# Transposing q, k and u by DMA in place of TensorE, with the sink loads on GpSimd's queue

## Chip, cores and metric

The kernel runs on one core of one Trainium2 chip. The metric is the device time of one execution in microseconds. A run counts as slow when it is over 1.5% above the fastest run of the same kernel. The engines are named as the profile names them: PE (TensorE), DVE (VectorE), ACT (ScalarE), POOL (GpSimd), SP (the queue of SyncE). To issue a DMA is to put it into a queue; it lands when its data have arrived.

## The reference

Attention with a sliding window of 128 and four sink tokens, followed by one MLP-Mixer block.

```python
# q, k, v: (batch 4, heads 8, seq 768, head_dim 64), float32
scores = scale * q @ k^T
keep = (key < 4) | ((query - key >= 0) & (query - key < 128))
x = softmax(where(keep, scores, -1e9)) @ v      # to (batch, 768, 512)
h  = relu(x^T @ w_tok1) @ w_tok2
u  = x + h^T
out = u + relu(u @ w_ch1) @ w_ch2
```

## The kernel before

Each batch has two groups of four heads (groups 0 to 7). PE runs the channel matmuls of batch b, called C1 and C2 here. The attention and the token mixing of batch b+1 are woven into them at fixed places of PE's program. Three operands must be transposed: q, k, and u, which C1 reads as `uT`. PE does all of that through PSUM, the memory in which PE's results stand, and ACT or DVE copies the result out; such a copy is called an eviction here.

```python
def load_qk(eng, src, dst, G, lo, hi):       # partition p holds tokens 6p..6p+5: rows of 1536 bytes
    return eng.dma_start(
        out=dst[:, lo:hi].rearrange("p h t d -> p h (t d)"),
        in_=src[G.b, G.h0 + lo:G.h0 + hi].rearrange("h (p t) d -> p h (t d)", t=NT))

def load_sinks():                            # four small loads on ACT's queue
    for h in range(GH):
        nc.scalar.dma_start(out=vs_f[4 * h:4 * h + 4, :, h, 0:D],
                            in_=v.rearrange("b (a h) s d -> h s (b a) d", h=GH)[h, 0:4])

def tr(j, which):                            # q or k of two heads: six PE transposes, one copy
    ps = ps_ms.tile([P, NT, P], BF16, name="ps_tr", tag="ms")
    for t in range(NT):
        nc.tensor.transpose(ps[:, t], src[:, j, t].rearrange("p i d -> p (i d)"), ident)
    ...
def utr(st):                                 # one 128-row block of u: four PE transposes, one copy
    ps = ps_ms.tile([P, NC, P], BF16, name="ps_ut", tag="ms")
    for c in range(NC):
        nc.tensor.transpose(ps[:, c], u_sb[:, st, ts(c, P)], ident)
    nc.scalar.activation(uT[:, :, ts(st, P)], ps, AF.Copy)

def prep_v(g):
    cast_v(held[g])
    if g + 2 < NG and g >= 2:
        fetch(g + 2)                         # loads of q, k, v for two groups later, on the SP queue
...
            # (cut) towards the end of batch b's channel matmuls:
            fill += [(mid + 0.01, lambda n=n: prep_qk(n)) for n in (h + 1, h + 2)]
            fill += [(mid + 0.01, lambda n=n: prep_v(n)) for n in (h + 1, h + 2)]
            hi = mid + 0.03                  # then token mixing and the transposes of u for batch b+1
            fill += [(hi + (0.97 - hi) * n / (len(nhead) - 1), f) for n, (f, _) in enumerate(nhead)]
```

The first half of C1 of a batch reads only the first three of the six blocks of `uT`.

The softmax here doesn't subtract the row's maximum and nothing guards it: scores larger than these inputs give would overflow.

## Time and profile before

| | |
|---|---|
| time, median | 242.3 us |
| PE busy, share of the span | 218.0 us, 91% |
| ACT, DVE, POOL busy | 43%, 47%, 38% |
| DMA packets, bytes | 39315, 29.40 MB |

The view by stretches gives the stretch and its length in us, the busy time of PE, of PE's weight loads, of DVE, ACT and POOL (with the number of instructions), then the granted PE clock as a share of full speed, the busy share of the DMA engines as the profile counts it, which can pass 1, and the rate in GB/s. From 80 us on PE is busy nearly all the time (two of the stretches are shown); at the start it is not.

```profile
7.00:12.00 5.00, 0.51 (x6) 0.34 (x6) 1.39 (x6) 1.68 (x2) 4.06 (x8) 0.60 1.11 345
12.00:19.00 7.00, 6.50 (x39) 3.03 (x40) 2.20 (x5) 3.48 (x5) 4.63 (x7) 0.56 1.20 189
...
90.00:100.00 10.00, 9.97 (x65) 5.20 (x64) 5.31 (x8) 2.83 (x6) 1.62 (x3) 1.00 1.15 319
100.00:110.00 10.00, 10.00 (x85) 5.86 (x82) 5.29 (x11) 7.47 (x12) 1.73 (x2) 1.00 0.82 203
```

The timeline of ACT (start, duration, engine, line, what) shows why the start is slow. The four sink-load issues hold ACT for 7.62 us, and its first cast of k comes only at 11.60 us. (The bracket calls these 10.30 us idle, since the profile does not count issues as busy.)

```profile
2.66 7.62 ACTq L127 DMA_DIRECT2D vs_f<-in_v_dram  x4
10.30 1.28 ACT L119 ACT_TABLE_LOAD   x1 [10.30 <-POOL qb L116]
11.60 0.84 ACT L119 ACTIVATE kb<-k_113 128x768 bf16<-128x768 f32 x1
```

The timeline of PE at the passage from batch 0 to batch 1 shows what a set of PE transposes costs. The six transposes of line 193 push the next C1 matmuls from 101.37 to 101.70 us, that is 0.33 us. Sets of four transposes of u, read in the same way a little earlier, cost 0.22 to 0.23 us.

```profile
101.37 0.50 PE L193 MATMUL ps_tr<-ident,qb 128*128 128x128 bf16 x6
101.70 0.81 PE L321 MATMUL ps_v<-uT,w_ch_103 128*128 128x384 bf16 x4
```

The timeline of the SP queue just before that passage is a list of DMA issues. Six loads for groups 6 and 7 are issued from 87.38 to 96.6 us.

```profile
87.38 0.39 SPq L98 DMA_DIRECT2D q_1238<-in_q_dram  x1
87.86 0.53 SPq L98 DMA_DIRECT2D k_1239<-in_k_dram  x1
90.19 0.37 SPq L122 DMA_DIRECT2D v_1242<-in_v_dram  x1
90.61 4.77 SPq L98 DMA_DIRECT2D q_1249<-in_q_dram  x1
95.43 0.55 SPq L98 DMA_DIRECT2D k_1250<-in_k_dram  x1
96.08 0.51 SPq L122 DMA_DIRECT2D v_1253<-in_v_dram  x1
```

### The profile page before, as it was taken

The page shows a single profiled execution, that of the slowest core. Times are in us where ns is not written, and L with a number is a line of the kernel's source. Part 1 is how long each engine was busy: PE and PEld are TensorE (multiplying, and loading weights), DVE is VectorE, ACT ScalarE, POOL GpSimd, SP SyncE. Part 2 cuts the span into 40 slices and gives each one's busy share as a digit, 9 for nine tenths or more (in the row PEclk, how much of TensorE's full clock was granted, in tenths as well). Part 3 has the DMA queues.
Part 4 walks back from the last instruction along what each step waited for, and adds up shares of the span by engine and source line. Part 5 has one row for each costly group of instructions (what it writes and reads, how often), then busy time and mean ns, then how long its engine had stood idle before and what let it go on. Part 6 is the DMA issues. An engine that isn't in the chain of part 4 may idle for free.

```text
span 240.4 us, 4233 instructions
## 1 busy us (share of the span) xinstructions
PE 218.0 (91%) x1733; PEld 121.6 (51%) x1733; DVE 113.6 (47%) x251; ACT 103.6 (43%) x162; POOL 91.3 (38%) x126
## 2 busy tenths in 40 slices
PE   6099895899889989999999999998999999999993
PEld 2044373355455654554565644655566555554441
DVE  3325566335475455562563645633556444333331
ACT  0248833343978412478572212596761123321100
POOL 6669407000498992018279900047390000000000
PEclk9659999799999999999999999999999999999999
DMA  6999999989207999990010112100001021101122
GB/s 221 350 214 143 209 329 207 301 156 284 90 0 141 316 263 311 326 222 0 3 44 3 44 44 76 59 0 3 17 29 44 3 87 44 45 3 44 44 89 87
DMA packets 39315, 29.40 MB, mean 122 GB/s; under 512 B 25664, under 2 KB 35648, under 8 KB 39296
## 3 DMA queue, kind: packets, MB, share of 16 engines
q1 hardware_dynamic: 33744, 20.71, 32.5%
q0 software_dynamic: 4448, 7.08, 13.3%
q10 hardware_dynamic: 1104, 1.34, 1.6%
q8 instruction: 13, 0.21, 0.4%
q14 instruction: 6, 0.05, 0.1%
HBM read 26.77 MB, written 6.29 MB: 138 GB/s over the span
## 4 chain that ended last, share of the span: by engine, by line
PE 67%; DVE 9%; issue 6%; DMA 6%; ACT 5%; POOL 4%; ACTq 0%; DVEq 0%; POOLq 0%
PE ps_w L333 26%; PE ps_v L321 21%; PE ps_u L309 4%; ACT pT L225 4%; DMA v_116<-in_v_dram 3%; PE ps_h L302 3%; PE ps_s L219 3%; DMA k_113<-in_k_dram 3%; PE ps_tr L193 3%; PE ps_ut L315 2%; DVE o L336 2%; DVE u_sb L310 2%; PE ps_o L257 1%; DVE qT L113 1%; PE ps_o L252 1%
## 5 line engine op out<-in xcount | busy, mean ns | idle before, releaser
L321 PE MATMUL ps_v<-uT,w_ch_103 128*128 128x384 bf16 x384 | 75.3, 328 | 2.3 <-ACT uT L316 0.7
L321 PEld LDWEIGHTS <-w_ch_103 128*128 128x128 bf16 x384 | 35.2, 98 | 29.3 <-issue 10.2
L225 ACT ACTIVATE pT<-ps_s 128x1024 bf16<-128x1024 f32 (+1 forms) x48 | 43.7, 962 | 8.0 <-PE ps_s L219 7.8
L229 POOL TENSOR_TENSOR pT<-pT,mask_92 128x512 bf16<-128x512 bf16 x12 | 13.8, 1152 | 65.4 <-ACT pT L225 65.4
L336 DVE TENSOR_TENSOR o<-ps_w,u_sb 128x512 f32<-128x512 f32 x24 | 16.6, 692 | 29.1 <-PE ps_w L333 29.0
L316 ACT ACTIVATE uT<-ps_ut 128x512 bf16<-128x512 bf16 x24 | 14.0, 596 | 34.1 <-PE ps_ut L315 34.1
L310 DVE TENSOR_TENSOR u_sb<-ps_u,x_b 128x512 bf16<-128x512 f32 x24 | 16.3, 687 | 21.8 <-PE ps_u L309 21.8
L236 POOL TENSOR_SCALAR_AFFINE_SELECT pT<-pT 128x640 bf16<-128x640 bf16 x24 | 18.3, 762 | 6.5 <-ACT pT L225 6.5
L270 DVE TENSOR_TENSOR x_b<-ps_o,rc 128x256 bf16<-128x256 f32 x42 | 17.8, 425 | 1.4
L333 PE MATMUL ps_w<-w_ch_104,v_111 128*128 128x512 bf16 x72 | 18.3, 379 | 0.0
L333 PE MATMUL ps_w<-w_ch_104,v_574 128*128 128x512 bf16 x72 | 18.3, 379 | 0.0
L333 PE MATMUL ps_w<-w_ch_104,v_1361 128*128 128x512 bf16 x72 | 18.3, 379 | 0.0
L113 DVE COPY qT<-ps_tr 128x768 bf16<-128x768 bf16 x16 | 15.3, 955 | 4.8 <-PE ps_tr L193 4.6
L219 PE MATMUL ps_s<-qT,kT 64*128 64x256 bf16 x192 | 15.7, 269 | 0.9 <-ACT pT L225 0.8
L333 PE MATMUL ps_w<-w_ch_104,v_2040 128*128 128x512 bf16 x72 | 16.0, 379 | 0.0
L239 POOL TENSOR_SCALAR_AFFINE_SELECT pT<-pT 128x512 bf16<-128x512 bf16 x24 | 15.5, 648 | 0.0
L257 PEld LDWEIGHTS <-pT 128*128 128x128 bf16 x192 | 13.9, 98 | 2.9 <-issue 0.4
L119 ACT ACTIVATE kT<-ps_tr 128x768 bf16<-128x768 bf16 x14 | 11.3, 809 | 8.7 <-PE ps_tr L193 8.6
L302 PE MATMUL ps_h<-x_b,w_tok_101 128*128 128x256 bf16 x96 | 13.4, 272 | 1.0 <-DVE x_b L270 0.5
L257 PE MATMUL ps_o<-va,pT 128*128 128x65 bf16 x168 | 14.3, 194 | 0.0
L269 DVE RECIPROCAL rc<-ps_o 128x4 f32<-128x4 f32 x42 | 7.5, 178 | 13.7 <-PE ps_o L261 8.4
L324 ACT ACTIVATE v_2040<-ps_v 128x384 bf16<-128x384 f32 x12 | 5.9, 490 | 16.9 <-PE ps_v L321 16.2
(125 smaller groups left out, 298.8 us busy)
## 6 DMA issues: line engine op xcount, KB each, us to landing
out_dram<-o SPq DMA_DIRECT2D x23, 256.0 KB, 2.3
w_ch_103<-in_moe_w_ch_dram POOLq DMA_DIRECT2D x2, 768.0 KB, 10.1
w_ch_104<-in_moe_w_ch_dram POOLq DMA_DIRECT2D x2, 768.0 KB, 18.9
k_113<-in_k_dram ACTq DMA_DIRECT2D x2, 384.0 KB, 5.5
q_112<-in_q_dram SPq DMA_DIRECT2D x2, 384.0 KB
q_118<-in_q_dram SPq DMA_DIRECT2D x2, 384.0 KB, 8.1
v_116<-in_v_dram SPq DMA_DIRECT2D x1, 768.0 KB, 7.9
v_122<-in_v_dram SPq DMA_DIRECT2D x1, 768.0 KB, 9.8
```

The source lines that it names most:

```text
L113: nc.vector.tensor_copy(out=o, in_=i)
L219: nc.tensor.matmul(ps[:, i, at:at + w], G.kT[j][ds(64 * i, 64), ts(kt, P)], G.qT[j][ds(64 * i, 64), ds(kt * P, w)], start=not first, stop= ...
L225: nc.scalar.activation(pT[:, :, 512 * u:512 * u + n], ps[:, :, 0:n], AF.Exp, scale=scale)
L236: nc.gpsimd.affine_select(out=cur, in_=cur, compare_op=ALU.is_ge, fill=0.0, base=0, pattern=[[0, NT - 1], [1, P]], channel_multiplier=-1)
L239: nc.gpsimd.affine_select(out=prv, in_=prv, compare_op=ALU.is_ge, fill=0.0, base=-1, pattern=[[0, NT - 2], [-1, P]], channel_multiplier=1)
L257: nc.tensor.matmul(o, pT[:, i, ds(256 * qt, P)], G.va[:, h, qt], start=(qt < 2 and h == 0), stop=(h == GH - 1 and qt == 0), skip_group_che ...
L270: nc.vector.tensor_tensor(out=x_b[:, qt, c0:c0 + GH * D].rearrange("p (h d) -> p h d", h=GH), in0=o[:, :, 0:D], in1=rc.to_broadcast([P, GH ...
L302: nc.tensor.matmul(ps, w_tok1[:, t, ts(tt, P)], x_b[:, t, ds(a * GH * D, GH * D)], start=(t == 0), stop=(t == NT - 1))
L310: nc.vector.tensor_tensor(out=u_sb[:, st], in0=ps, in1=x_b[:, st], op=ALU.add)
L321: nc.tensor.matmul(ps, w_ch1[:, c, ts(ft, P)], uT[:, c, ds(half * HS, HS)], start=(c == 0), stop=(c == NC - 1))
L333: nc.tensor.matmul(ps, v1[:, ft, ts(st, P)], w_ch2[:, ft], start=(ft == 0), stop=(ft == NF - 1))
L336: nc.vector.tensor_tensor(out=o, in0=ps, in1=u_sb[:, st], op=ALU.add)
```

## The change

The intent is to take 168 transposes (96 of q and k, 72 of u) and their PSUM copies off PE, ACT and DVE, and to free ACT at the start. The PSUM copy also put the tokens of q and k into order; the DMA transpose, as it is written here, does not. So q and k of groups 4 to 7 are now loaded as 256-byte rows, in the layout that v always had. (Not shown below: the tiles of qT and kT now hold a whole group, with two buffers in place of three.)

```diff
+        G.dma = g >= 2 * GB
 def load_qk(eng, src, dst, G, lo, hi):
-            in_=src[G.b, G.h0 + lo:G.h0 + hi].rearrange("h (p t) d -> p h (t d)", t=NT))
+            in_=src[G.b, G.h0 + lo:G.h0 + hi].rearrange("h (p t) d -> p h (t d)", t=NT)
+        ) if not G.dma else eng.dma_start(
+            out=dst.rearrange("p h t d -> p (h t) d"),
+            in_=src[G.b, G.h0:G.h0 + GH].rearrange("h (t p) d -> p (h t) d", p=P))
...
+    def cast_and_turn(G, which, copy):
+        (cut: one cast on POOL to bf16, token block outermost)
+        nc.sync.dma_start_transpose(out=T, in_=flat)
...
 def load_sinks():
-            nc.scalar.dma_start(
-                out=vs_f[4 * h:4 * h + 4, :, h, 0:D],
+            nc.gpsimd.dma_start(out=vs_c[4 * h:4 * h + 4],
...
 def cast_sinks(lo, hi):      # the zeros of vsink now come from a small mask dm
-        nc.vector.tensor_copy(out=vsink[0:4 * GH, lo:hi], in_=vs_f[:, lo:hi])
+        for h in range(GH):
+            nc.vector.tensor_scalar(out=vsink[0:4 * GH, lo:hi, h, 0:D], in0=vs_c[:, lo:hi],
+                scalar1=dm[:, h], scalar2=None, op0=ALU.mult)
+            nc.vector.tensor_copy(out=vsink[0:4 * GH, lo:hi, h, D:D1],
+                in_=dm[:, h:h + 1].to_broadcast([4 * GH, hi - lo, 1]))
...
+        def sink_keys(j):       # used in place of tr() for groups 4 to 7
+            for i in range(2):
+                nc.scalar.activation(kz[j][ds(64 * i, 64), ds(8 * j + 4 * i, 4)],
+                                     G.T[1][j][ds(64 * i, 64), 0, 0:4], AF.Copy)
...
 def utr(st):
+            if b > 0:
+                nc.sync.dma_start_transpose(out=uT[:, :, ts(st, P)], in_=u_sb[:, st])
+                return
...
+                order += [(lambda g=g: begin(g), 0)] + ([(lambda h=h: begin(h), 0)] if b > 0 else [])
+                if held[g].dma:
+                    order += [(step(x, 0, i), 0) for x in (g, h) for i in range(2)]
```

The last lines put the sink-key copies of both groups at the start of batches 1 and 2 (for the attention of batches 2 and 3).

More of the change, by code (lines that the diff above doesn't have):

```diff
@@ L50 @@
     bfp = ctx.enter_context(tc.tile_pool(name="bfp", bufs=2))
-    att = ctx.enter_context(tc.tile_pool(name="att", bufs=3))
+    att = ctx.enter_context(tc.tile_pool(name="att", bufs=2))
     ptp = ctx.enter_context(tc.tile_pool(name="ptp", bufs=4))
@@ L65 @@
     ks = [[singles.tile([P, P], BF16, name=f"ks{a}{j}") for j in range(2)] for a in range(2)]
-    vs_f = singles.tile([4 * GH, NG, GH, D1], FP32, name="vs_f")
+    dm = singles.tile([4 * GH, GH, 1], FP32, name="dm")
+    vs_c = singles.tile([4 * GH, NG, D], FP32, name="vs_c")
     vsink = singles.tile([P, NG, GH, D1], BF16, name="vsink")
@@ L92, in tiles @@
         G.va = bfp.tile([P, GH, NT, D1], BF16, name="va")
-        G.qT, G.kT, G.pT = [None, None], [None, None], [None, None]
+        G.T, G.pT = [None, None], [None, None]
         return G
@@ L110, in cast @@
         copy(dst[:, j].rearrange("p t i d -> p i t d"), src[:, 2 * j:2 * j + 2])
+    def cast_and_turn(G, which, copy):
+        src, dst = ((G.q32, G.qb), (G.k32, G.kb))[which]
+        flat = dst.rearrange("p j t i d -> p (j t i d)")
+        copy(flat.rearrange("p (t h d) -> p t h d", t=NT, h=GH), src.rearrange("p h t d -> p t h d"))
+        T = att.tile([P, 2 * NT, P], BF16, name="qT" if which == 0 else "kT")
+        nc.sync.dma_start_transpose(out=T, in_=flat)
+        G.T[which] = [T.rearrange("d (t j) p -> d t j p", j=2)[:, :, j] for j in range(2)]
     def by_dve(o, i):
@@ L126, in load_sinks @@
         for h in range(GH):
-            nc.scalar.dma_start(
-                out=vs_f[4 * h:4 * h + 4, :, h, 0:D],
-                in_=v.rearrange("b (a h) s d -> h s (b a) d", h=GH)[h, 0:4])
+            nc.gpsimd.dma_start(out=vs_c[4 * h:4 * h + 4],
+                                in_=v.rearrange("b (a h) s d -> h s (b a) d", h=GH)[h, 0:4])
     def load_tok():
@@ L166, in build_sinks @@
     def build_sinks():
-        one = vs_f[:, :, :, D]
-        nc.gpsimd.memset(one, 1.0)
+        nc.gpsimd.memset(dm, 1.0)
         nc.gpsimd.affine_select(
-            out=one, in_=one, compare_op=ALU.is_ge, fill=0.0,
-            base=0, pattern=[[0, NG], [-4, GH]], channel_multiplier=1)
+            out=dm[:, :, 0], in_=dm[:, :, 0], compare_op=ALU.is_ge, fill=0.0,
+            base=0, pattern=[[-4, GH]], channel_multiplier=1)
         nc.gpsimd.affine_select(
-            out=one, in_=one, compare_op=ALU.is_ge, fill=0.0,
-            base=3, pattern=[[0, NG], [4, GH]], channel_multiplier=-1)
+            out=dm[:, :, 0], in_=dm[:, :, 0], compare_op=ALU.is_ge, fill=0.0,
+            base=3, pattern=[[4, GH]], channel_multiplier=-1)
     def cast_sinks(lo, hi):
-        nc.vector.tensor_copy(out=vsink[0:4 * GH, lo:hi], in_=vs_f[:, lo:hi])
+        for h in range(GH):
+            nc.vector.tensor_scalar(
+                out=vsink[0:4 * GH, lo:hi, h, 0:D], in0=vs_c[:, lo:hi],
+                scalar1=dm[:, h], scalar2=None, op0=ALU.mult)
+            nc.vector.tensor_copy(
+                out=vsink[0:4 * GH, lo:hi, h, D:D1],
+                in_=dm[:, h:h + 1].to_broadcast([4 * GH, hi - lo, 1]))
     def cast_v(G):
@@ L193, in tr @@
                 nc.tensor.transpose(ps[:, t], src[:, j, t].rearrange("p i d -> p (i d)"), ident)
-            dst = att.tile([P, S], BF16, name="qT" if which == 0 else "kT")
+            if j == 0:
+                T = att.tile([P, 2 * NT, P], BF16, name="qT" if which == 0 else "kT")
+                G.T[which] = [T[:, NT * x:NT * x + NT] for x in range(2)]
+            dst = G.T[which][j].rearrange("d t p -> d (t p)")
             (by_act if which and (g >= GB or j == g) else by_dve)(
                 dst.rearrange("d (p t) -> d p t", t=NT), ps.rearrange("d t p -> d p t"))
-            if which == 0:
-                G.qT[j] = dst
-            else:
-                G.kT[j] = dst
+            if which == 1:
                 for i in range(2):
@@ L219, in sc @@
                     nc.tensor.matmul(
-                        ps[:, i, at:at + w],
-                        G.kT[j][ds(64 * i, 64), ts(kt, P)], G.qT[j][ds(64 * i, 64), ds(kt * P, w)],
+                        ps[:, i, at:at + w].rearrange("p (c q) -> p c q", q=P),
+                        G.T[1][j][ds(64 * i, 64), kt], G.T[0][j][ds(64 * i, 64), kt:kt + w // P],
                         start=not first, stop=not first or at > 0, skip_group_check=first)
@@ L245, in sk @@
             for j in range(2):
-                nc.tensor.matmul(ps, kz[j], G.qT[j][:, 2 * P:S], start=(j == 0), stop=(j == 1))
+                nc.tensor.matmul(ps.rearrange("p (c q) -> p c q", q=P), kz[j], G.T[0][j][:, 2:NT], start=(j == 0), stop=(j == 1))
             G.pk = small.tile([P, 512], BF16, name="pk")
@@ L284, in pv2 @@
                 in0=o[:, :, :, 0:D], in1=rc.to_broadcast([P, 2, GH, D]), op=ALU.mult)
-        T = [lambda j=j, w=w: tr(j, w) for j in range(2) for w in range(2)]
+        if G.dma:
+            T = [lambda j=j: sink_keys(j) for j in range(2)]
+        else:
+            T = [lambda j=j, w=w: tr(j, w) for j in range(2) for w in range(2)]
         Sc = [lambda j=j, u=u: sc(j, u) for j in range(2) for u in range(3)]
@@ L393, in prep_qk @@
         def prep_qk(g, by=(by_pool, by_pool)):
+            if held[g].dma:
+                for which in range(2):
+                    cast_and_turn(held[g], which, by_pool)
+                return
             for j in range(2):
@@ L413 @@
         parts[1] = attention(1, G1, xs[0], True)
-        nc.gpsimd.memset(vs_f, 0.0)
         load_q(G0, 0, 2)
@@ L420 @@
         load_k(G1, 0, 2, nc.scalar)
-        load_sinks()
         nc.vector.memset(warm, 0.0)
@@ L428 @@
         build_masks()
+        load_sinks()
+        build_sinks()
         nc.vector.memset(vsink, 0.0)
@@ L462 @@
         seq += [C(G1, 0, 0, by_pool), C(G1, 0, 1, by_pool), I(1), step(0, 1, 3), step(1, 0, 0), step(0, 1, 4)]
-        seq += [step(1, 0, 1), step(0, 1, 5), step(1, 1, 0), build_sinks]
+        seq += [step(1, 0, 1), step(0, 1, 5), step(1, 1, 0)]
         seq += [C(G1, 1, 0, by_pool), C(G1, 1, 1, by_pool), step(0, 2, 0), step(1, 0, 2), step(1, 1, 1), step(1, 0, 3)]
@@ L482 @@
                     order += [(lambda: prep_qk(2), 0)]
-                order += [(lambda g=g: begin(g), 0)]
-                order += [(step(g, 0, i), 8) for i in range(4)]
+                order += [(lambda g=g: begin(g), 0)] + ([(lambda h=h: begin(h), 0)] if b > 0 else [])
+                if held[g].dma:
+                    order += [(step(x, 0, i), 0) for x in (g, h) for i in range(2)]
+                else:
+                    order += [(step(g, 0, i), 8) for i in range(4)]
                 for n in range(3):
@@ L489 @@
                     order += [(lambda: prep_qk(3, (by_dve, by_act)), 0)]
-                order += [(lambda h=h: begin(h), 0)]
-                order += [(step(h, 0, i), 8) for i in range(4)]
+                order += [(lambda h=h: begin(h), 0)] if b == 0 else []
+                if not held[h].dma:
+                    order += [(step(h, 0, i), 8) for i in range(4)]
                 if b == 0:
```

## The prediction

> **What bounds the kernel now.** TensorE is 91% busy (page); PE holds 67% of the chain of waits. The stretch view shows PE busy 9.1 to 10 of every 10 us from 80 to 230 us, at full clock. Before that it is not PE alone: from 7.7 to 12.5 us PE waits for ACT's first cast of k, and ACT was idle until 10.3 us because its four sink-load issues (timeline, 2.66 to 10.28 us) blocked it; PE then ran at clock 0.5 until 19 us.
>
> **Removed.** 96 PE transposes of q and k, 72 of u. The groups view books about 90 ns each, but in the timeline six delay the next matmul by 0.33 us (101.37 to 101.70), four by about 0.22. So 16 x 0.33 + 18 x 0.22 = about 9.3 us of PE time, nearly all on the critical path: 1.3 us before batch 1's channel matmuls, 8 after. The evictions that go were hidden. Moving the sink loads lets PE restart about 4 us earlier; the split sink casts on DVE give some back: 3.5 us net.
>
> **Added.** q and k of groups 4 to 7 are loaded as 256-byte rows, as v is. By the stretch view v loads run at about 218 GB/s (10 to 18 us), the old q/k loads at 390 (80 to 82 us): 3.6 us for 768 KB in place of 2.0. Loads, DMA transposes and stores sit on the SP queue in program order: before batch 1's u transposes come three stores, four q/k transposes (waiting for GpSimd's casts), then six loads for groups 6 and 7. In the old trace the third store ends at 87.3 us, the casts at 88.6, and the faster loads last until 107 us. PE's u transposes needed no DMA; now they do. The Trainium skill, "DMA: Bandwidth & Descriptors" (Two DMAs through the same engine are not ordered), says descriptors of one queue start in order; the old trace agrees in that one SP load issue took 4.77 us behind others.
>
> Estimate: casts done at 86 us; four transposes 6 to 8 us of queue (same page, Latency and other measured facts, 261 GB/s: 1.5 us per 384 KB; no transpose is in the old trace); six loads 21.6 us; a store and three u transposes: uT lands at about 116 us. PE would be ready at 100.7 - 3.5 - 1.3 = 96 us, and waits for exactly those three u transposes. Stall 20 us, plus 2 for a clock drop after it. Batches 2 and 3 have no loads queued and 4 to 5 us of slack: little stall.
>
> Sum: 242.3 - 9.3 - 3.5 + 20 + 2 = about 251; I say 249.
>
> **Prediction: 249 us, 231 to 264 in 8 of 10; faster 0.2, same 0.14, slower 0.66.**
>
> **What would show it.** PE idle 10 to 25 us once, near 96 to 116 us, ended by a DMA into uT; first ACT cast near 7 to 8 us instead of 11.6; q/k loads of groups 4 to 7 at about 218 GB/s; batches 1 and 2 about 4 us shorter each.
>
> **What would make it wrong.** If the u transposes do not queue behind the loads, or the loads run near 390 GB/s, the stall vanishes: about 230 us. If a DMA transpose takes 5 us or more, batches 2 and 3 stall too: 265 us and more. If the start is bound by v's landing (15.8 us), not by ACT, its 3.5 us do not come.

## The result

The changed kernel takes 257.09 us (255.85 to 258.43, 4 runs), the kernel before 242.31 us. The ratio of the fast runs is 1.061, 95% interval 1.0556 to 1.0664. Ratios here are the mean time of one kernel's fast runs over that of the other's of the same rounds, so they are not quite the ratio of the medians that are quoted.

The view by stretches of the changed kernel, with the same columns as before. The start is at full clock. From 94 us on PE does nothing, while the DMA engines run at 218 GB/s.

```profile
7.00:12.00 5.00, 4.58 (x46) 2.06 (x45) 3.23 (x7) 3.87 (x5) 3.85 (x5) 1.00 1.10 327
12.00:19.00 7.00, 6.54 (x63) 2.98 (x62) 3.63 (x9) 6.51 (x9) 4.08 (x6) 1.00 1.25 205
...
90.00:100.00 10.00, 3.93 (x19) 1.56 (x16) 3.01 (x5) 0.00 (x0) 0.00 (x0) 0.94 1.24 214
100.00:110.00 10.00, 0.00 (x0) 0.00 (x0) 0.00 (x0) 0.00 (x0) 0.00 (x0) 0.50 1.34 218
```

The timeline of ACT at the start: the first cast of k now stands at 5.36 us, 6.2 us earlier.

```profile
2.38 1.28 ACT L132 ACT_TABLE_LOAD   x1 [2.38 <-issue]
5.36 0.84 ACT L132 ACTIVATE kb<-k_114 128x768 bf16<-128x768 f32 x1 [1.70 <-DMA k_114<-in_k_dram]
```

The timeline of the SP queue at the passage to batch 1: four q/k transposes, six loads, a store, and only then, at 112.64 us, the first transpose of u.

```profile
83.30 1.78 SPq L122 DMA_TRANSPOSE qT<-qb  x1
85.19 2.52 SPq L122 DMA_TRANSPOSE kT<-kb  x1
87.81 1.45 SPq L122 DMA_TRANSPOSE qT<-qb  x1
89.36 1.64 SPq L122 DMA_TRANSPOSE kT<-kb  x1
91.06 0.98 SPq L103 DMA_DIRECT2D q_1248<-in_q_dram  x1
92.09 2.54 SPq L103 DMA_DIRECT2D k_1249<-in_k_dram  x1
94.73 3.47 SPq L135 DMA_DIRECT2D v_1252<-in_v_dram  x1
98.25 3.55 SPq L103 DMA_DIRECT2D q_1259<-in_q_dram  x1
101.84 3.55 SPq L103 DMA_DIRECT2D k_1260<-in_k_dram  x1
105.50 3.50 SPq L135 DMA_DIRECT2D v_1263<-in_v_dram  x1
109.09 3.46 SPq L371 DMA_DIRECT2D out_dram<-o  x1
112.64 2.52 SPq L340 DMA_TRANSPOSE uT<-u_sb  x2
```

The timeline of PE at the same place: the wait for `uT` before C1 of batch 1.

```profile
92.04 1.89 PE L362 MATMUL ps_w<-w_ch_105,v_112 128*128 128x512 bf16 x8
118.53 1.44 PE L350 MATMUL ps_v<-uT,w_ch_104 128*128 128x384 bf16 x4 [24.60 <-DMA uT<-u_sb]
```

A ledger can be made from the start of each batch's first C1 matmul in the two timelines of PE. For the changed kernel, PE is ready for batch 1 at 118.53 - 24.60 = 93.93 us.

| stretch | before, us | after, us | difference | predicted |
|---|---|---|---|---|
| start to C1 of batch 0 | 43.21 | 37.48 | -5.7 | -3.5 |
| batch 0, until PE is ready for batch 1 | 57.51 | 56.45 | -1.1 | -1.3 |
| wait for uT | 0 | 24.60 | +24.6 | +20 |
| batch 1 | 51.01 | 49.68 | -1.3 | -4, and +2 of low clock |
| batch 2 | 50.99 | 50.56 | -0.4 | -4 |
| batch 3 and end | 37.7 | 37.8 | +0.1 | 0 |
| span | 240.4 | 256.6 | +16.2 | +9 |

The stall is as foretold in kind. The surprise is in batches 1 and 2. The table of PE's waits after 80 us (who waited for whom, total us, times, longest) shows C1 waiting for ACT for 3.3 us in batch 2 and 2.1 us in batch 1; before, the last two lines, it was 0.5 us in each.

```profile
PE ps_v L350 <- DMA uT<-u_sb: 24.6, 1, 24.6
PE ps_v L350 <- ACT v_1341 L353: 3.3, 3, 1.9
PE ps_v L350 <- ACT v_584 L353: 2.1, 3, 0.7
PE ps_v L321 <- ACT v_1361 L324: 0.5, 1, 0.5
PE ps_v L321 <- ACT v_574 L324: 0.5, 1, 0.5
```

The timeline of ACT at the start of batch 2 shows what ACT does meanwhile. Eight sink-key copies (from 169.63 to 171.36 us, 1.73 us) and two exps stand between the first and the second eviction of C1's PSUM.

```profile
169.11 0.49 ACT L353 ACTIVATE v_1341<-ps_v 128x384 bf16<-128x384 f32 x1 [13.42 <-DVE o L365]
169.63 0.42 ACT L225 ACTIVATE ks_95<-kT 64x4 bf16<-64x4 bf16 x2
170.06 0.42 ACT L225 ACTIVATE ks_96<-kT 64x4 bf16<-64x4 bf16 x2
170.49 0.42 ACT L225 ACTIVATE ks_97<-kT 64x4 bf16<-64x4 bf16 x2
170.92 0.42 ACT L225 ACTIVATE ks_98<-kT 64x4 bf16<-64x4 bf16 x2
171.36 1.94 ACT L248 ACTIVATE pT<-ps_s 128x1024 bf16<-128x1024 f32 x2
173.19 0.50 ACT L353 ACTIVATE v_1341<-ps_v 128x384 bf16<-128x384 f32 x1
```

### The profile page after: what moved, and what is told of

The parts are those of the page before. It is cut to its first block, busy times and chain, and to the rows that moved or that the text cites. A ratio compares the mean times of both kernels' runs of the same rounds, so it can differ in the third digit from the quotient of the medians.

```text
span 256.6 us, 3888 instructions
## 1 busy us (share of the span) xinstructions
PE 210.2 (82%) x1547; PEld 112.7 (44%) x1565; DVE 107.0 (42%) x241; ACT 91.1 (36%) x152; POOL 91.1 (36%) x121
## 4 chain that ended last, share of the span: by engine, by line
PE 57%; SPq 12%; ACT 10%; DVE 8%; DMA 6%; POOL 3%; issue 2%; DVEq 0%; ACTq 0%; POOLq 0%
PE ps_v L350 20%; PE ps_w L362 18%; ACT pT L248 7%; SPq L103 4%; DMA v_948<-in_v_dram 4%; PE ps_s L242 3%; PE ps_u L335 3%; SPq L135 3%; PE ps_h L328 3%; DMA uT<-u_sb 2%; PE ps_warm L468 2%; SPq L122 2%; SPq L371 2%; PE ps_tr L211 2%; SPq L340 2%
## 5 line engine op out<-in xcount | busy, mean ns | idle before, releaser
L350 PE MATMUL ps_v<-uT,w_ch_104 128*128 128x384 bf16 x384 | 77.6, 338 | 31.1 <-DMA uT<-u_sb 24.6
L350 PEld LDWEIGHTS <-w_ch_104 128*128 128x128 bf16 x384 | 36.6, 100 | 62.8 <-issue 42.9
L355 DVE TENSOR_SCALAR v_584<-ps_v 128x384 bf16<-128x384 f32 x12 | 6.7, 557 | 38.9 <-PE ps_v L350 38.9
L353 ACT ACTIVATE v_584<-ps_v 128x384 bf16<-128x384 f32 x12 | 5.9, 494 | 42.7 <-PE ps_v L350 42.6
L362 PE MATMUL ps_w<-w_ch_105,v_584 128*128 128x512 bf16 x69 | 17.5, 379 | 0.2
L362 PE MATMUL ps_w<-w_ch_105,v_1341 128*128 128x512 bf16 x69 | 17.5, 379 | 0.2
L362 PE MATMUL ps_w<-w_ch_105,v_112 128*128 128x512 bf16 x68 | 17.3, 379 | 0.2
L353 ACT ACTIVATE v_1922<-ps_v 128x384 bf16<-128x384 f32 x12 | 5.9, 491 | 29.7 <-PE ps_v L350 16.2
L362 PE MATMUL ps_w<-w_ch_105,v_1922 128*128 128x512 bf16 x70 | 15.9, 379 | 0.1
L280 PE MATMUL ps_o<-va,pT 128*128 128x65 bf16 x168 | 14.9, 194 | 0.0
L353 ACT ACTIVATE v_1341<-ps_v 128x384 bf16<-128x384 f32 x12 | 5.9, 493 | 22.3 <-DVE o L365 13.4
```

What stands on the lines that cost most here:

```text
L280: nc.tensor.matmul(o, pT[:, i, ds(256 * qt, P)], G.va[:, h, qt], start=(qt < 2 and h == 0), stop=(h == GH - 1 and qt == 0), skip_group_che ...
L350: nc.tensor.matmul(ps, w_ch1[:, c, ts(ft, P)], uT[:, c, ds(half * HS, HS)], start=(c == 0), stop=(c == NC - 1))
L353: nc.scalar.activation(v1[:, ft, ds(half * HS, HS)], ps, AF.Relu)
L362: nc.tensor.matmul(ps, v1[:, ft, ts(st, P)], w_ch2[:, ft], start=(ft == 0), stop=(ft == NF - 1))
```

## The experiments

There are two questions: what makes the 24.6 us, and where the 8 us that batches 1 and 2 should have saved went. Each label below is a kernel. Unless said otherwise, it is the changed kernel with the edit shown.

### late_loads: the six loads after the u transposes

```diff
-            if g + 2 < NG and g >= 2:
+            if g in (2, 3):
                 fetch(g + 2)
...
+                if b == 0:
+                    fill += [(0.98, lambda n=n: fetch(n)) for n in (6, 7)]
```

> Changed kernel, but the six loads for groups 6 and 7 are issued on the SP queue after batch 1's six u transposes, not before. Theory A (the 24.6 us stall is the u transposes standing behind six 3.6 us loads in SP's program order): the stall shrinks to 0 to 3 us, what the four q/k transposes ahead leave, and the half-clock stretch after it goes too; 231 to 236 us, so faster than the kernel before. Rival B (the transposes themselves are slow, or the eight-deep reuse of DMA semaphores holds them): PE still waits over 8 us for uT, 242 us or more.

Measured: 237.17 us, ratio to before 0.979 (0.972 to 0.986), correct. The wait for `uT` fell from 24.6 to 4.9 us, more than theory A's 3 and less than rival B's 8. The time missed the expected range by 1.2 us.

```profile
PE ps_v L350 <- DMA uT<-u_sb: 4.9, 1, 4.9
```

By the timelines, what is left comes from the four q/k transposes. DVE has written the third block of u by 89.8 us, but the q/k transposes hold SP until 92.6 us, and the third transpose of u is issued only at 97.0 us. The position of the six loads on the SP queue therefore costs about 20 us.

### gp_loads: the loads in place, but on GpSimd's queue

```diff
-            load_q(G, 0, GH)
-            load_k(G, 0, GH)
-            load_v(G)
+            eng = nc.gpsimd if g >= 6 else nc.sync
+            load_q(G, 0, GH, eng)
+            load_k(G, 0, GH, eng)
+            load_v(G, eng)
```

> Changed kernel, the six loads stay at their place in the program but are issued by GpSimd on its own queue. Theory A (order on the SP queue): the u transposes are issued near 90 us and share the 16 DMA engines with the loads, so they land within some 3 to 8 us; stall 2 to 8 us, 234 to 242 us. Rival C (what counts is that the DMA engines are full with 256-byte rows, on whatever queue): the stall stays above 15 us, 250 us or more.

Measured: 263.80 us over all four runs, 262.91 us without a slow one of 273.78, which is left out of the ratio too; ratio 1.088 (1.079 to 1.097), correct. Theory A's figure failed clearly: the wait for `uT` grew to 30.1 us. Rival C's figures came true, but whether the short rows are the reason is not shown: long rows were not tried on GpSimd's queue. The order on SP is not the whole mechanism. The timeline of the SP queue shows what happened: now the q/k transposes themselves are slow, and the transposes of u still stand behind them.

```profile
84.74 10.05 SPq L122 DMA_TRANSPOSE kT<-kb  x1
94.90 16.75 SPq L122 DMA_TRANSPOSE qT<-qb  x1
111.76 4.77 SPq L122 DMA_TRANSPOSE kT<-kb  x1
...
117.25 2.55 SPq L340 DMA_TRANSPOSE uT<-u_sb  x2
```

### gp_loads_u1: the same, with u of batch 1 by PE

The edit is that of gp_loads with `if b > 1` in `utr`. This takes the u transposes out of that place, so that the q/k transposes alone show.

> u1_pe with the six loads issued by GpSimd, as in gp_loads. Theory G (a DMA transpose gets little of the DMA engines beside bulk loads of GpSimd's queue, so the q/k transposes themselves come late, on top of any order on SP): issues of the later q/k transposes take 5 us and more as in gp_loads, the sink-key copies on ACT wait for group 5's kT, and PE stalls 15 to 22 us though u is by PE: 250 to 257 us. Rival (in gp_loads only the order on SP ahead of u mattered): 234 to 238 us.

Measured: 266.99 us (one run). Theory G holds in kind, and its size was too small. PE waited 26.1 us for group 4's kT and another 6.0 us for ACT, which waited for group 5's.

```profile
PE ps_s L242 <- DMA kT<-kb: 26.1, 1, 26.1
PE ps_v L350 <- ACT v L353: 10.6, 6, 6.0
```

The view by stretches shows that the engines were not moving data at their usual rate towards the end. The DMA share is still 1.19, but the rate is 58 GB/s from 110 to 120 us.

```profile
110.00:120.00 10.00, 0.00 (x0) 0.00 (x0) 0.00 (x0) 0.00 (x0) 0.00 (x0) 0.50 1.19 58
```

So a DMA transpose on SP beside bulk loads on GpSimd's queue is served late and slowly. The packet records of the kept traces show two phases. In gp_loads, from 90 to 108 us, GpSimd's queue moved 912 packets of 4096 bytes (207 GB/s) while SP's transposes moved 1004 packets of 256 bytes (14 GB/s). In the changed kernel transposes alone moved 281 GB/s (86.5 to 88.5 us). The near-equal counts fit two queues that take turns packet by packet, which leaves the one with small packets little; no run tested this apart. Later, in gp_loads_u1 from 110 to 120 us, the packets themselves became slow: 855 ns for one of 4096 bytes, against 314 ns from 90 to 104 us. Why, stays open; no run here tells it.

### wide_rows: the old 1536-byte rows

```diff
-        ) if not G.dma else eng.dma_start(
-            out=dst.rearrange("p h t d -> p (h t) d"),
-            in_=src[G.b, G.h0:G.h0 + GH].rearrange("h (t p) d -> p (h t) d", p=P))
+        )
```

> Changed kernel with the old 1536-byte rows for the q and k loads of groups 4 to 7; the tokens then stand in another order, so the result is wrong on purpose. Theory A with the row length as its measure: four of the six loads in the queue take 2.0 in place of 3.6 us, so the stall falls by about 6.5 us, from 24.6 to 17 to 19, and the time to 249 to 252 us. If the row length does not matter, 256 us; if it is all of it, under 240 us.

Measured: 251.35 us (one run), with a wait for `uT` of 17.7 us, both in the expected range. `uT` arrived at 112.94 us in place of 118.53 us, so the row length accounts for 5.6 us of its lateness; PE was also ready 1.3 us later in this run. The comparison with the reference passed, although q and k of batches 2 and 3 have their tokens in another order. With the reference's input the scores are small (q and k are drawn with a spread of 0.1, and the scores then have one of 0.01) and the softmax nearly even, so the comparison does not see such an error. It is not a usable version, and "correct" says little of the q/k path in the other runs either.

### u1_pe: u of batch 1 by PE

```diff
-            if b > 0:
+            if b > 1:
                 nc.sync.dma_start_transpose(out=uT[:, :, ts(st, P)], in_=u_sb[:, st])
```

> Changed kernel, but u of batch 1 is transposed by PE again as before; q/k of groups 4 to 7 and u of batches 2 and 3 stay with the DMA. Theories A and C: the 24.6 us stall goes, 1.3 us of PE transposes come back, and about 2 us of half clock go: 231 to 235 us. Rival D (batch 1 waits for its q and k as well, which also come by DMA): a wait of 5 us or more for kT stays, 240 us or more.

Measured: 234.52 us, ratio 0.969 (0.963 to 0.975), correct, in the expected range. There is no wait for a DMA after 80 us. Rival D fell: batch 1's q/k transposes, the last of them issued from 90.17 to 91.85 us, arrive in time. One line thus turns a loss of 6.1% into a gain of 3.1%. But 6.5 us of waits for ACT are left in this kernel:

```profile
PE ps_v L350 <- ACT v L353: 6.5, 6, 1.9
```

### qk_pe_u123: q and k by PE, u of batches 1 to 3 by DMA

```diff
-        G.dma = g >= 2 * GB
+        G.dma = False
```

> u of batches 1 to 3 by DMA, all of q and k by PE, with the old 1536-byte rows; the six loads keep their place ahead of batch 1's u transposes on the SP queue, and no q/k transpose is in that queue. Theory A: the stall stays but is smaller, since the loads alone last until about 101 us (107 in the old trace less the start's 6) and PE is ready at about 93 us: wait of 8 to 12 us for uT, 240 to 247 us. Rival (the q/k transposes are what holds uT): no wait over 3 us, about 232 us.

Measured: 243.08 us, ratio 1.004 (1.000 to 1.008), correct. The wait for `uT` is 10.2 us. With no q/k transpose in the queue and with the old fast rows, the six loads alone still hold `uT` back, as theory A says. The arrival of `uT` in three runs gives the parts of the stall: 102.75 us with the loads alone, those of q and k in long rows, 112.94 us with the four q/k transposes and their casts ahead of them (wide_rows), 118.53 us with the short rows too (the changed kernel). Differences of 1 to 2 us between runs in the start are contained in these.

### sinks_only: the sink part alone on the kernel before

The edit is the `load_sinks`, `build_sinks` and `cast_sinks` of the change, nothing else.

> The kernel before with the sink-load part of the change alone (loads on GpSimd's queue, the small mask and the split casts), all transposes by PE. Theory: ACT's early blocking is the whole of the start's gain, 5.7 us in the trace of the changed kernel, and it carries to the end: 235.5 to 238 us. Rival (the start is bound by the landing of v, or the gain needs the DMA transposes): 241 us or more.

Measured: 236.12 us, ratio 0.977 (0.971 to 0.982), correct, in the expected range. The sink part alone is worth 6.1 us. Its first C1 matmul starts at 35.77 us, and batches 1 and 2 take 51.0 us each as before.

### u1_old_sinks: the DMA transposes without the sink part

The edit is u1_pe with the old sink functions.

> The opposite: u1_pe (DMA transposes of q/k of groups 4 to 7 and of u of batches 2 and 3, u of batch 1 by PE) with the old sink loads on ACT's queue. If the parts add up, the DMA transposes are worth only 242.3 - 5.7 - 234.5 = 2 us: 239 to 241.5 us. If they are worth the 7.9 us of PE time that they take off: 234 to 235 us.

Measured: 239.88 us, ratio 0.992 (0.987 to 0.996), correct, in the expected range. With the stall gone, the DMA transposes take 16 x 0.33 + 12 x 0.22 = 7.9 us off PE, and yield 2.4 us.

### qk_pe_u23: only u of batches 2 and 3 by DMA

The edit is `G.dma = False` and `if b > 1`.

> u1_pe with q and k of all batches transposed by PE (old row loads, old order of steps), so only u of batches 2 and 3 by DMA. Theory E: q/k by DMA pays nothing net, as its 5.3 us of PE time come back as ACT waits and half clock: 242.3 - 5.7 - 2.6 = 234 us, 233 to 235.5, the same as u1_pe. If q/k by DMA did pay its 5.3 us, this kernel is 5 us slower than u1_pe, 239 us.

Measured: 233.65 us, ratio 0.966 (0.961 to 0.971), correct, in the expected range and as fast as u1_pe (234.52 us). Transposing q and k by DMA as the change does it has no net gain, although it takes 5.3 us off PE.

### u1_pool_keys: the sink keys on GpSimd

```diff
-                nc.scalar.activation(kz[j][ds(64 * i, 64), ds(8 * j + 4 * i, 4)],
-                                     G.T[1][j][ds(64 * i, 64), 0, 0:4], AF.Copy)
+                nc.gpsimd.tensor_copy(out=kz[j][ds(64 * i, 64), ds(8 * j + 4 * i, 4)],
+                                      in_=G.T[1][j][ds(64 * i, 64), 0, 0:4])
```

The base is u1_pe.

> u1_pe with the eight small sink-key copies at the start of batches 1 and 2 (1.74 us together) done by GpSimd in place of ACT. Theory E (the PE time saved in batches 1 and 2 is lost because these copies stand ahead of two exps and hold back ACT's evictions for the channel matmuls): the 1.86 and 1.89 us waits fall to 0.6 or less, and a half-clock stretch may go: 230 to 232.5 us against 234.5. Rival F (it is the exps themselves, not the copies): waits stay above 1.3 us, 234 us or more.

Measured: 227.56 us (226.70 to 229.80), ratio 0.942 (0.937 to 0.947), correct. It beats both kernels, and is 2.4 us faster than expected. The waits for ACT fell from 6.5 to 2.7 us, the longest from 1.9 to 0.7 us:

```profile
PE ps_v L350 <- ACT v L353: 2.7, 4, 0.7
```

Its batches 1 and 2, read as in the ledger, take 47.28 and 47.25 us. That is 3.7 us less than before in each, about the 4 us that the prediction gave. So theory E holds: the PE time was saved and then lost to the eight small copies on ACT. In the profiled runs the two kernels are 233.0 - 227.6 = 5.4 us apart. Batch 1 is 1.8 us shorter than in u1_pe, as long as the copies took, and batch 2 3.3 us. The waits make 3.8 us of it. A half-clock stretch that u1_pe has at 150 to 154 us (clock 0.57) is missing here and fits the rest, but was not tested apart.

### late_poolkeys: the whole change with both mends

The edits are those of late_loads and of u1_pool_keys.

> The whole change (u of batch 1 by DMA too) with the two mends: the six loads after batch 1's u transposes, and the sink keys copied by GpSimd. Expected: late_loads' 237.2 less the 5 to 7 us that the GpSimd copies gave u1_pe: 230 to 232.5 us, with a wait for uT of 4 to 5 us left. Rival: u by DMA is as good as by PE in batch 1: 227 to 228.5 us, as u1_pool_keys.

Measured: 231.20 us, ratio 0.954 (0.951 to 0.957), correct, in the expected range; the wait for `uT` is 4.1 us. Against late_loads, from which it differs by the copies alone, batch 1 is 1.2 us shorter (48.52 for 49.68) and batch 2 1.9 us (47.25 for 49.12). In batch 1, u by PE (1.3 us) is cheaper than u by DMA as long as the q/k transposes stand ahead of it: u1_pool_keys is 3.6 us faster, though the two also place the six loads differently. The best version found is u1_pool_keys.

## Why the prediction was wrong

The direction, the stall, its place and its cause were foretold, and 257.1 us lies in the stated range. The size was wrong: 6.7 us slower was forecast, 14.8 us slower was measured. That it is not further off is in part luck: two terms were too favourable by 4.3 and 4.6 us, and the start, which was taken too low by 2.2 us, hides some of that.

- **The step that failed first** is "16 x 0.33 + 18 x 0.22 = about 9.3 us of PE time, nearly all on the critical path: 1.3 us before batch 1's channel matmuls, 8 after", with "batches 1 and 2 about 4 us shorter each". The 1.3 us came (1.1). In the place of -4 + 2 - 4 = -6 us for batches 1 and 2, low clock included, the trace shows -1.3 - 0.4 = -1.7 us, most of the miss in batch 2. The time was taken off PE. But the change also puts eight sink-key copies on ACT at the start of each of these batches, 1.73 us in a row ahead of two exps, and C1 waits there for ACT's eviction. The prediction counted what left ACT and not what came to it. u1_pool_keys shows it: with these copies on GpSimd each batch is 3.7 us shorter than before. The copies are not all of batch 2's miss. late_loads has them too, and the same 1.9 us wait, but no half clock after it: its batch 2 takes 49.12 us. So about 1.9 us go to the copies (late_poolkeys), and the other 1.4 us of the changed kernel's 50.56 go with its half clock from 174.0 to 177.4 us.
- **The second term that was mis-sized is the stall**: called 20 us, it is 24.6 us. PE was ready 2.1 us earlier than foretold (93.9 against 96 us), and `uT` came 2.5 us later (118.5 against 116). The four q/k transposes took 91.06 - 83.30 = 7.8 us of the queue (6 to 8 foretold). The loads ran at 218 GB/s, as foretold. The tail of a store and three u transposes, which the sum hardly counted, took from 112.6 to 118.5 us.
- **The start** gained 5.7 us in the trace and 6.1 us by itself (sinks_only), not 3.5. PE's first transposes of k stand at 6.6 us in place of 12.5, so 5.9 us earlier and not 4. From 7 to 19 us PE also has the clock 1.00 in place of 0.56 to 0.60. How much the clock adds to the earlier start was not tested apart. The start also scatters: in the eleven profiled kernels that have the new sink loads, the first C1 matmul stands anywhere from 35.2 to 38.5 us.
- These add up: +4.3 us from the two batches, +4.6 from the stall, -2.2 from the start and some tenths are the 7 us between the foretold sum of +9.2 and the trace's +16.2. The 249 us of the forecast was another 2 us below that sum.
- **The low clock after the stall** came as foretold: 0.50 until after 122 us, in the changed kernel's view by stretches of 1 us.
- **The mechanism was half right.** The prediction said that the u transposes queue behind the loads on SP. late_loads, u1_pe and qk_pe_u123 bear that out. But "if the u transposes do not queue behind the loads ... the stall vanishes" is refuted by gp_loads. On another queue the same loads starve the q/k transposes instead, and the stall is longer. Nor is the old row length of q and k enough: a stall of 17.7 us is left (wide_rows). What must be right is the time at which bulk loads run, not only their queue.
- **The figure drawn from the Trainium skill**, "DMA: Bandwidth & Descriptors", Latency and other measured facts (261 GB/s for a DMA transpose), gave 1.5 us for each 384 KB. Four issues took 7.8 us of the SP queue, 1.9 us each or 203 GB/s worked out, still within the 6 to 8 us foretold. That does not refute the page: until about 86 us the packets of three stores shared the engines, and of the transposes alone the trace's packets give 281 GB/s from 86.5 to 88.5 us and 208 GB/s from 89.5 to 91 us.

## What to carry to other kernels

Before moving work from an engine to a DMA queue, list what already stands in that queue ahead of it at the moment of need: a latency that cost nothing while only prefetches used the queue becomes a stall of PE. Cost what a change adds to each engine at the point where it stands, not only what it removes; eight copies of 0.2 us ahead of a PSUM eviction, with the half clock that came after one of the waits, undid most of what the transposes gave. And split a change into its parts before judging it: here the small part, the sink loads, carried 6.1 us of gain, and the large part hid behind one bad place in a queue.

## What the Trainium skill lacked or had wrong

- "DMA: Bandwidth & Descriptors", Rules for kernel authors, says that "A transpose next to ordinary DMAs needs nothing". That row speaks of corrupted results. It does not speak of time: beside six loads of 768 KB on GpSimd's queue, three of the four issues of 384 KB transposes on SP took 4.8 to 18.9 us in place of 1.5 to 2.5 (gp_loads, gp_loads_u1), and the core's DMA rate fell to 58 GB/s over 10 us (gp_loads_u1). No page gives a figure for this.
- The same page, Latency and other measured facts, gives 261 GB/s for a DMA transpose with a non-contiguous middle dimension; whether the ones here count as such was not settled. Here transposes that had the engines to themselves moved 208 to 281 GB/s, so the figure is not shown wrong. The page lacks what a kernel waits for: a transpose of 128x512 bf16 (128 KB) took 1.2 us to issue and 2.5 us (median) from issue to landing.
- The same page, Issuing engines are not separate DMA queues, calls the sequencer's issue time "usually small relative to the DMA itself". Behind other loads an issue took as long as the transfer: 3.5 us for each of the last four 768 KB loads on SP. On ACT, behind three loads of k, four 8 KB loads took 7.62 us to issue and held up ACT's computing.
- "TensorE: Matmul & The Clock Gate", Part 1, says that PE falls to half rate after at least one idle window of about 3.4 us. In the changed kernel a PE wait of 1.90 us at 171.8 us was followed by half clock from 174.0 to 177.4 us. In u1_pe a wait of 1.86 us was followed by full clock and one of 1.89 us by 0.57. So a wait below 3.4 us can be enough, but need not be.
